# A one-core decode kernel: the query weights split into two loads, and the MLP weights issued from another engine's queue

## The chip, the cores and the metric

The kernel runs on one core of a Trainium2 chip. The metric is the device time of one launch in microseconds (us); three runs of the kernel before gave 1302.87, 1302.97 and 1303.05 us, median 1302.97. All times below that carry a position ("at 31.44") are counted from the first instruction of the profiled execution.

## The reference

One decode step for two sequences (B = 2) with model width 512:

```
xn  = layernorm(x)                                  # x: [2, 1, 512]
q   = (xn @ wq) -> 32 heads of 128                  # wq: [512, 4096], 8.4 MB
s   = softmax(q k^T / sqrt(128)) v, then @ wo       # k, v: [2, 8 kv heads, 32768, 128]
g   = silu( relu(xn @ w1 + b1)^2 @ w2 + b2 )        # w1: [512, 1792], w2: [1792, 512]
out = x + s * g
```

Everything is float32. The key and value caches are 537 MB together; wq is 8,388,608 bytes, w1 and w2 together 7,340,032, wo 8,388,608. Each byte is read once.

## The kernel before, in words

**Buffers.** Two slots of 128 partitions x 16384 floats (8.4 MB each) take the large loads in turn. A load is one DMA of 128 rows, one row for each partition. The output weights wo have their own buffer, `wo_sb`.

**The stream of loads.** All large loads are issued by SyncE (the row name is SPq) through `load` (L164 to L171), in this order: wq into slot 0, wm (w1 and w2 side by side, 14336 floats to a row) into slot 1, and then for each of the 16 pairs of sequence and kv head two key loads (`kt`) and two value loads (`vt`), 64 loads of 8.4 MB in all, which alternate between the slots. At the end follow six pieces of wo. The first two loads need no wait (L173). Every later one waits until TensorE has read the slot's previous contents: `release` (L178) records TensorE's token and calls `load` for the next entry of the list, so the order in which TensorE finishes with the slots is the order in which SyncE issues. Load i+2 is thus issued when load i has been consumed, while load i+1 is on its way.

**Ahead of the stream.** Behind the first two loads SyncE runs `AHEAD` = 9 semaphore clears on a semaphore that is not yet in use (L174), which move its later instructions by nine places and do nothing else.

**The front of the program**, in TensorE's order: layernorm in a few small matmuls; q = xn @ wq as 32 matmuls (L252 to L258: 4 blocks d of 128 rows of wq, each with 8 matmuls into two PSUM banks), which wait for the whole of wq; the release of slot 0, which lets SyncE issue the first key load; transposes of q; then `mlp` (L295), which waits for wm, does 16 + 14 matmuls with VectorE work between them, and releases slot 1, which lets SyncE issue the second key load. Each float32 matmul shows as two records in the profile, so the 32 matmuls of q are x64 there.

**ScalarE** issues three tiny loads at the start (`small`, and `xb` twice), does one copy and a square root for the layernorm (L244), and then waits for TensorE's 32 matmuls before it copies q out of PSUM (L262).

**The loop** runs over the 16 pairs on TensorE, ScalarE and VectorE: scores from two key loads, softmax, and the value products from two value loads. TensorE's work for one load takes about 9 us. `release` is called at the end of each load's matmuls (L291, L384).

Tokens are pairs of a semaphore and a value; `wait` (L42) puts a wait ahead of the engine's next instruction. `fetch` (L58) is a DMA issued by the engine itself, in its own order of instructions. Every operation of TensorE, ScalarE and VectorE is recorded by one helper, so they all carry L64 in the profile.

Of the kernel before, what the change touches and what calls it, by code (L numbers as in the profile page):

```python
# [16 lines left out]
B, D, HQ, HKV, SK, DH, F = 2, 512, 32, 8, 32768, 128, 1792  # L17
REP = HQ // HKV
NS = B * HKV
ND = D // P  # L20
# [5 lines left out]
FJ = FG // 32  # L26
SLOT = HALF
NSLOT = 2
PIECES = (16, 8, 5, 2)
WIDE = 24  # L30
AHEAD = 9
HN = P // 2
SCALE = 1.0 / math.sqrt(DH)

# [91 lines left out]
def build(nc, x22, x8, kt, vt, wq, wm, wo, out):  # L126
    pe, act, dve = (Looped(nc, e, n) for e, n in ((nc.tensor, "pe"), (nc.scalar, "act"), (nc.vector, "dve")))
    pool, sp = (Engine(nc, e, n) for e, n in ((nc.gpsimd, "pool"), (nc.sync, "sp")))

    def mm(*args, **kw):  # L130
        pe.do("matmul", *args, **kw)
# [4 lines left out]
    def sb(name, *shape):  # L136
        return nc.alloc_sbuf_tensor(name, [P, *shape], F32)

    slots = [sb(f"slot{i}", SLOT) for i in range(NSLOT)]
# [10 lines left out]
    small, xs, xc, sq, st = sb("small", P), sb("xs", 22), sb("xc", 8), sb("sq", 8), sb("st", 16)  # L150
# [5 lines left out]

    slot_sem = [nc.alloc_semaphore(f"slot{i}") for i in range(NSLOT)]
    piece_sem = [nc.alloc_semaphore(f"piece{i}") for i in range(len(PIECES) + 2)]
    small_sem, xe_sem, out_sem = (nc.alloc_semaphore(n) for n in ("small", "xe", "out"))
    count = [0] * NSLOT  # L160
    free = [None] * NSLOT
    issued = [0]

    def load(src, width):  # L164
        i = issued[0] % NSLOT
        issued[0] += 1
        if free[i] is not None:
            sp.wait(free[i])
        count[i] += 16
        nc.sync.dma_start(slots[i][:, 0:width], src).then_inc(slot_sem[i], 16)  # L170
        return i, (slot_sem[i], count[i])  # L171

    stream = [load(wq, SLOT), load(wm, 2 * FJ * D)]  # L173
    for _ in range(AHEAD):  # L174
        nc.sync.sem_clear(out_sem)
    todo = [(x[s, u], SLOT) for s in range(NS) for x in (kt, vt) for u in range(2)]
# [16 lines left out]
    t = pool.done(g.memset(ident[:, :], 0.0))  # L193
# [12 lines left out]
    for u in range(2):  # L206
# [5 lines left out]
    t = dve.done("tensor_reduce", selh[:, :], ident[:, :].rearrange("p (a h) -> p h a", h=REP), axis=AX.X, op=ALU.add)  # L212
    dve.wait(t)
    t_seln = dve.done("tensor_scalar", seln[:, :], selh[:, :], -SCALE, None, op0=ALU.mult)
    t_selg = dve.done("tensor_reduce", selg[:, :].rearrange("p (r y) -> p r y", r=2),
                      ident[:, None, :].to_broadcast([P, 2, P]).rearrange("p r (g y) -> p r y g", g=NG), axis=AX.X, op=ALU.add)
# [6 lines left out]
    t = pe.done()  # L223
    dve.wait(t)
    t = dve.done("tensor_copy", xs[:, :], ms[:, 0:22])
    pe.wait(t, t_one)
    mm(ms[:, 32:40], mean[:, :], xs[:, 0:8], start=True, stop=True)
    t = pe.done()
    dve.wait(t)
    t = dve.done("tensor_reduce", st[:, 2:4], ms[:, 32:40].rearrange("p (d b) -> p b d", b=B), axis=AX.X, op=ALU.add)  # L230
    dve.wait(t)
    t = dve.done("tensor_tensor", xc[:, :].rearrange("p (d b) -> p d b", b=B), xs[:, 0:8].rearrange("p (d b) -> p d b", b=B),
                                 st[:, None, 2:4].to_broadcast([P, ND, B]), op=ALU.add)
    dve.wait(t)
    t = dve.done("tensor_mul", sq[:, :], xc[:, :], xc[:, :])
    pe.wait(t)
    mm(ms[:, 64:72], mean[:, :], sq[:, :], start=True, stop=True)
    t = pe.done()
    dve.wait(t)
    t = dve.done("tensor_reduce", st[:, 4:6], ms[:, 64:72].rearrange("p (d b) -> p b d", b=B), axis=AX.X, op=ALU.add)  # L240
    dve.wait(t)
    t = dve.done("tensor_scalar", st[:, 6:8], st[:, 4:6], -1.0, 1e-5, op0=ALU.mult, op1=ALU.add)
    act.wait(t)
    t = act.done("activation", st[:, 8:10], st[:, 6:8], AF.Sqrt)  # L244
    dve.wait(t)
    t = dve.done("reciprocal", st[:, 10:12], st[:, 8:10])
    dve.wait(t)
    t_x = dve.done("tensor_tensor", xT[:, :, 0:B], xc[:, :].rearrange("p (d b) -> p d b", b=B),
                                   st[:, None, 10:12].to_broadcast([P, ND, B]), op=ALU.mult)


    i, t = stream[0]  # L252
    pe.wait(t_x, t, t_selg)
    for d in range(ND):
        for f in range(2):
            for c in range(NG):
                lo = d * HQ * DH + (f * NG + c) * W
                mm(sc[f][32 * c:32 * c + 32, :], xT[:, d, :], slots[i][:, lo:lo + W], start=(d == 0), stop=(d == ND - 1))  # L258
    t = pe.done()
# [3 lines left out]
    for f in range(2):  # L263
# [3 lines left out]
        t = pe.done()  # L267
# [14 lines left out]
    def scores(u):  # L282
        i, t = stream[0]
        pe.wait(t, t_set, t_exp[u])
        for j in range(NJ):
            for c in range(NG):
                lo = (c * NJ + j) * W
                mm(sc[u][32 * c:32 * c + 32, :], qz[:, 28 - 4 * j:60 - 4 * j], slots[i][:, lo:lo + W],
                         start=(j == 0), stop=(j == NJ - 1))
        t = pe.done()  # L290
        release(t)  # L291
        dve.wait(t)
        return t, dve.done("tensor_reduce", rm[:, u:u + 1], sc[u][:, :], axis=AX.X, op=ALU.max)
# [44 lines left out]
    for s in range(NS):  # L338
# [4 lines left out]
        t_s, t = scores(1)  # L343
# [3 lines left out]
        t = dve.done("tensor_reduce", r1[:, :], rm[:, :], axis=AX.X, op=ALU.max)  # L347
        pe.wait(t, *([t_rs] if t_rs else []))
        tr(ms[:, :P], r1[:, :].to_broadcast([P, P]), ident[:, :])
        t = pe.done()  # L350
        dve.wait(t)
        t = dve.done("tensor_reduce", mh[:, :], ms[:, :P].rearrange("p (a h) -> p h a", h=REP), axis=AX.X, op=ALU.max)
        dve.wait(t)
        t = dve.done("tensor_mul", mm4[:, :], mh[:, :], seln[:, :])
        dve.wait(t)
        t = dve.done("tensor_reduce", nm[:, :], mm4[:, :], axis=AX.X, op=ALU.add)
# [5 lines left out]
        for u in range(2):  # L362
# [3 lines left out]
            t = pe.done()  # L366
# [4 lines left out]
        t = pe.done()  # L371
        dve.wait(t)
        t_rs = dve.done("reciprocal", rs[:, :], ms[:, :REP])
        for u in range(2):
            i, t = stream[0]
            pe.wait(t, t_pT[u], t_osb)
            for n in range(32):
                y = n % NG
                k, r = divmod(n, 8)
                lo = k * 32 + r * 4  # L380
# [7 lines left out]
        for n in range(4):  # L388
            lo = n * (P - REP)
# [19 lines left out]
    first = True  # L409
# [8 lines left out]
    for n, sem in zip(PIECES, piece_sem):  # L418
        if h == WIDE:
            pe.wait(t_w)  # L420
            for u in range(2):
                for c in range(NG):
                    lo = c * P + u * HN
                    mm(acc[32 * c:32 * c + 32, 0:2 * HN:2], selg[:, 32 - u:64 - u], o_sb[:, lo:lo + HN], start=(u == 0), stop=False)
        pe.wait((sem, 16))
        for h in range(h, h + n):
            if h < WIDE:
                c = h % NG
                mm(wb[32 * c:32 * c + 32, :], heads(h, 0), wt[:, h, :], start=(h < NG), stop=(h >= WIDE - NG))
                if h == WIDE - 1:  # L430
                    t = pe.done()
# [12 lines left out]
    t = pe.done()  # L444
    dve.wait(t, t_gate)
    t = dve.done("tensor_tensor_scan", yb[:, :], gate[:, :], acc[:, :2 * HN], 0.0, op0=ALU.mult, op1=ALU.add)
    sp.wait(t)
    nc.sync.dma_start(out, yb[:, :]).then_inc(out_sem, 16)
    used = sorted(x.num for x in [e.sem for e in (pe, act, dve, pool, sp)] + slot_sem + piece_sem + [small_sem, xe_sem])
    nc.sync.sem_clear(range(used[0], used[-1] + 1))  # L450
    nc.sync.wait_ge(out_sem, 16)
    for e in (pe, act, dve):
# [48 lines left out]
```

## Time and profile before

| | before |
|---|---|
| median of three runs | 1302.97 us |
| the profiled execution's own time | 1302.98 us |
| its span, first to last instruction | 1301.7 us |
| DMA queue of SyncE (q1) | 10512 packets, 561.06 MB, busy 99.7% of 16 engines' span |
| DMA queue of ScalarE (q10) | 65 packets, 0.02 MB |
| instruction queue q8 | 5 packets, 0.08 MB |
| TensorE busy | 672.9 us (52%) |
| VectorE, ScalarE, GpSimd busy | 49.5, 79.1, 5.6 us |

The core has 16 DMA engines. A queue's share is the time that its packets took, over 16 spans. A "row" of a load below is the part of one partition, 64 KB for a full slot. The page's chain names what each engine waited for last; the DMA issue rows tell how long after its issue a load had landed.

### The profile page before, as it was taken

What the parts mean: (1) busy time and instruction counts of PE and PEld (TensorE: products, weight loads), DVE (VectorE), ACT (ScalarE), POOL (GpSimd) and SP (SyncE); (2) the same over time, 40 slices, a digit from 0 to 9 for tenths busy, and PEclk for the clock granted to TensorE, in tenths of its full rate; (3) what the DMA queues carried; (4) which work ended last, traced back from release to release, by engine and by line L of the source; (5) the groups of instructions that cost most, each with busy time, mean ns of one, the idle gap of its engine ahead of it and who ended that gap; (6) DMA issues with size and microseconds to landing.
All of it is one profiled execution on the core that took longest, in us unless ns stands there. A gap on an engine that the chain in (4) does not pass through costs nothing.

```text
span 1301.7 us, 10377 instructions
## 1 busy us (share of the span) xinstructions
PE 672.9 (52%) x4713; PEld 208.6 (16%) x4713; DVE 49.5 (4%) x165; ACT 79.1 (6%) x139; POOL 5.6 (0%) x30
## 2 busy tenths in 40 slices
PE   3445445535536545545645545554654654554565
PEld 1111111211112111111211111121111211111122
DVE  0000000000000000000000000000000000000000
ACT  1010010100001010010101001010010101001010
POOL 0000000000000000000000000000000000000000
PEclk9777677678677778667677767767767767767777
DMA  9999999999999999999999999999999999999998
GB/s 412 428 446 425 443 425 445 419 443 427 429 441 427 443 427 443 423 445 421 443 427 427 443 427 443 427 443 421 445 423 441 429 427 443 427 443 425 445 421 363
DMA packets 10583, 561.17 MB, mean 431 GB/s; under 512 B 1195, under 2 KB 1617, under 8 KB 1745
## 3 DMA queue, kind: packets, MB, share of 16 engines
q1 hardware_dynamic: 10512, 561.06, 99.7%
q8 instruction: 5, 0.08, 0.0%
q10 hardware_dynamic: 65, 0.02, 0.0%
q14 instruction: 1, 0.01, 0.0%
HBM read 561.01 MB, written 0.07 MB: 431 GB/s over the span
## 4 chain that ended last, share of the span: by engine, by line
DMA 75%; PE 24%; issue 1%; DVE 0%; ACT 0%; SPq 0%; ACTq 0%
DMA slot<-in_vt 36%; DMA slot<-in_kt 36%; PE sc L64 12%; PE o_ps L64 11%; DMA slot<-in_wm 3%; PE wb L64 1%; DVE hT L64 0%; ACT o_sb L64 0%; DVE o_sb L64 0%; PE ot L64 0%; DVE yb L64 0%; SPq L170 0%; ACT sc L64 0%; ACTq L454 0%; ACTq L102 0%
## 5 line engine op out<-in xcount | busy, mean ns | idle before, releaser
L64 PE MATMUL sc<-slot,qz 128*32 128x512 f32 x2048 | 295.5, 742 | 299.6 <-DMA slot<-in_kt 299.6
L64 PE MATMUL o_ps<-slot,pT 128*16 128x512 f32 x2048 | 294.4, 739 | 209.0 <-DMA slot<-in_vt 209.0
L64 PEld LDWEIGHTS sc<-slot,qz 128*32 128x32 f32 x2048 | 81.0, 133 | 503.3 <-issue 503.3
L64 PEld LDWEIGHTS o_ps<-slot,pT 128*16 128x16 f32 x2048 | 69.3, 113 | 420.7 <-issue 420.7
L64 ACT ACT_TABLE_LOAD x19 | 24.4, 1283 | 650.3 <-DVE nm L64 647.3
L64 PE MATMUL tp<-ident,prob 128*128 128x128 f32 x136 | 31.2, 403 | 53.2 <-ACT prob L64 53.2
L64 DVE TENSOR_REDUCE rm<-sc 128x1 f32<-128x512 f32 x32 | 22.1, 691 | 574.9 <-PE sc L64 574.9
L64 ACT COPY o_sb<-o_ps 128x512 f32<-128x512 f32 x16 | 9.4, 586 | 504.8 <-PE o_ps L64 504.8
L64 PEld LDWEIGHTS tp<-ident,prob 128*128 128x128 f32 x136 | 24.0, 206 | 57.7 <-issue 55.7
L64 DVE TENSOR_REDUCE t<-ot 128x4 f32<-128x64 f32 x16 | 3.6, 224 | 524.2 <-PE ot L64 524.2
L64 ACT ACTIVATE prob<-sc,nm 128x512 f32<-128x512 f32 x32 | 21.7, 683 | 0.2
L64 ACT COPY pT<-tp 128x512 f32<-128x512 f32 x32 | 18.8, 586 | 13.8 <-PE tp L64 13.8
L64 PE MATMUL sc<-slot,xT 128*32 128x512 f32 x64 | 8.6, 695 | 17.7 <-DMA slot<-in_wq 17.7
L64 PE MATMUL ot<-ident,o_sb 128*128 128x128 f32 x64 | 10.1, 280 | 13.7 <-ACT o_sb L64 12.8
L64 PEld LDWEIGHTS ms<-selh,l 128*128 128x128 f32 x64 | 15.6, 334 | 0.0
L64 PE MATMUL ms<-ident,r 128*128 128x128 f32 x16 | 4.7, 294 | 20.0 <-DVE r L64 20.0
L64 PE MATMUL ms<-selh,l 128*128 128x4 f32 x64 | 13.7, 319 | 0.0
L64 PEld LDWEIGHTS ot<-ident,o_sb 128*128 128x128 f32 x64 | 6.7, 141 | 27.9 <-issue 27.9
L64 PE MATMUL wb<-slot,xT 128*32 128x448 f32 x32 | 4.8, 762 | 6.4 <-DMA slot<-in_wm 6.4
L275 POOL COPY qz<-qT 128x4 f32<-128x4 f32 x16 | 3.0, 187 | 1167.2 <-PE sc L64 1137.2
L64 PEld LDWEIGHTS ms<-ident,r 128*128 128x128 f32 x16 | 2.1, 133 | 34.1 <-issue 34.1
L64 ACT ACTIVATION_READ_ACCUMULATOR prob<-sc,nm 128x1 f32 x32 | 6.3, 196 | 0.0
(63 smaller groups left out, 55.4 us busy)
## 6 DMA issues: line engine op xcount, KB each, us to landing
slot<-in_wm SPq DMA_DIRECT2D x1, 7168.0 KB, 38.4
wo_sb<-in_wo SPq DMA_DIRECT2D x1, 4096.0 KB, 39.1
wo_sb<-in_wo SPq DMA_DIRECT2D x1, 2048.0 KB, 43.5
wo_sb<-in_wo SPq DMA_DIRECT2D x1, 1280.0 KB, 45.8
slot<-in_kt SPq DMA_DIRECT2D x32, 29.1
slot<-in_vt SPq DMA_DIRECT2D x32, 29.1
wo_sb<-in_wo SPq DMA_DIRECT2D x1, 512.0 KB, 46.6
wo_sb<-in_wo SPq DMA_DIRECT2D x2, 128.0 KB, 46.4
```

The lines of the kernel that those rows point to most:

```text
L64: instruction = getattr(self.e, name)(*[x(i) if callable(x) else x for x in args], **kw)
L275: return pool.done(g.tensor_copy(qz[:, 28:32], qT[:, b, hkv, :]))
```

## The change

wq is loaded in two parts into the same slot: the first 12288 floats of each row (`FIRST`, the blocks d = 0 to 2) with a semaphore of its own, `first_sem`, and the last 4096 floats (block d = 3) with slot 0's semaphore. Both are issued by SyncE, one behind the other. The load wm, which SyncE issued second, is now issued by ScalarE: behind the square root, ScalarE waits until the first part of wq has landed and then issues wm into slot 1. TensorE waits for `first_sem` ahead of its first 24 matmuls and for slot 0's semaphore ahead of the last 8. SyncE runs 8 semaphore clears in place of 9. The 64 cache loads and the pieces of wo stay as they were, on SyncE.

```diff
-AHEAD = 9
+AHEAD = 8
+FIRST = 3 * SLOT // 4
...
-    stream = [load(wq, SLOT), load(wm, 2 * FJ * D)]
+    for lo, hi, sem in ((0, FIRST, first_sem), (FIRST, SLOT, slot_sem[0])):
+        nc.sync.dma_start(slots[0][:, lo:hi], wq[:, lo:hi]).then_inc(sem, 16)
+    stream = [(i, (slot_sem[i], 16)) for i in range(2)]
+    issued[0] = 2
+    count[0:2] = 16, 16
     for _ in range(AHEAD):
         nc.sync.sem_clear(out_sem)
...
     t = act.done("activation", st[:, 8:10], st[:, 6:8], AF.Sqrt)
+    act.wait((first_sem, 16))
+    act.fetch(slot_sem[1], slots[1][:, 0:2 * FJ * D], wm)
...
-    pe.wait(t_x, t, t_selg)
+    pe.wait(t_x, (first_sem, 16), t_selg)
     for d in range(ND):
+        if d == ND - 1:
+            pe.wait(t)
         for f in range(2):
```

SyncE's instructions at the start of its program, before:

```order
L170 DMA slot<-in_wq 128x16384 [waits barrier_Pool_Activation_PE_DVE_SP_release]
L170 DMA slot<-in_wm 128x14336
L175 ISA x9
L170 DMA slot<-in_kt 128x16384 [waits pe] x2
L170 DMA slot<-in_vt 128x16384 [waits pe] x2
```

and now (the lines are those of the changed file):

```order
L175 DMA slot<-in_wq 128x12288 [waits barrier_Pool_Activation_PE_DVE_SP_release]
L175 DMA slot<-in_wq 128x4096
L180 ISA x8
L171 DMA slot<-in_kt 128x16384 [waits pe] x2
L171 DMA slot<-in_vt 128x16384 [waits pe] x2
```

The load of wm has left SyncE's order, the load of wq has become two, and one clear (ISA) is gone; the cache loads follow as before.

ScalarE's instructions from the layernorm to the gate of the MLP, before:

```order
L64 ACTIVATE st<-st 128x2 [waits dve]
L64 COPY prob<-sc 128x512 [waits pe]
L64 COPY prob<-sc 128x512
L64 COPY o_sb<-wb 128x512 [waits pe]
L64 ACT_TABLE_LOAD
L64 ACTIVATE gate<-yb 128x64 [waits dve]
```

and now:

```order
L65 ACTIVATE st<-st 128x2 [waits dve]
L65 DMA slot<-in_wm 128x14336 [waits first]
L65 COPY prob<-sc 128x512 [waits pe]
L65 COPY prob<-sc 128x512
L65 COPY o_sb<-wb 128x512 [waits pe]
L65 ACT_TABLE_LOAD
L65 ACTIVATE gate<-yb 128x64 [waits dve]
```

Between the square root (`ACTIVATE st`) and the copies of q (`COPY prob`) stands the load of wm, with a wait for the first part of wq.

TensorE's instructions around the query projection (`sc<-slot,xT`), before:

```order
L64 MATMUL ms<-sq,mean 128x8 [waits dve]
L64 MATMUL sc<-slot,xT 32x512 [waits slot0,dve]
L64 MATMUL sc<-slot,xT 32x512 x31
L64 MATMUL tp<-ident,prob 128x128 [waits act]
L64 MATMUL tp<-ident,prob 128x128 x3
```

and now:

```order
L65 MATMUL ms<-sq,mean 128x8 [waits dve]
L65 MATMUL sc<-slot,xT 32x512 [waits first,dve]
L65 MATMUL sc<-slot,xT 32x512 x23
L65 MATMUL sc<-slot,xT 32x512 [waits slot0]
L65 MATMUL sc<-slot,xT 32x512 x7
L65 MATMUL tp<-ident,prob 128x128 [waits act]
L65 MATMUL tp<-ident,prob 128x128 x3
```

The one wait for wq has become two, 24 matmuls behind the first and 8 behind the second; the matmuls themselves and their order are the same.

More of the change, by code (lines that the diff above doesn't have):

```diff
@@ L158, in build @@
     piece_sem = [nc.alloc_semaphore(f"piece{i}") for i in range(len(PIECES) + 2)]
-    small_sem, xe_sem, out_sem = (nc.alloc_semaphore(n) for n in ("small", "xe", "out"))
+    small_sem, xe_sem, first_sem, out_sem = (nc.alloc_semaphore(n) for n in ("small", "xe", "first", "out"))
     count = [0] * NSLOT
@@ L448, in build @@
     nc.sync.dma_start(out, yb[:, :]).then_inc(out_sem, 16)
-    used = sorted(x.num for x in [e.sem for e in (pe, act, dve, pool, sp)] + slot_sem + piece_sem + [small_sem, xe_sem])
+    used = sorted(x.num for x in [e.sem for e in (pe, act, dve, pool, sp)] + slot_sem + piece_sem + [small_sem, xe_sem, first_sem])
     nc.sync.sem_clear(range(used[0], used[-1] + 1))
```

## The prediction

> **What bounds the kernel now.** I read the DMA rows of the page first, since a kernel that reads 561 MB once can hardly be bound by anything else.
>
> ```profile
> span 1301.7 us, 10377 instructions
> DMA  9999999999999999999999999999999999999998
> q1 hardware_dynamic: 10512, 561.06, 99.7%
> q8 instruction: 5, 0.08, 0.0%
> HBM read 561.01 MB, written 0.07 MB: 431 GB/s over the span
> DMA 75%; PE 24%; issue 1%; DVE 0%; ACT 0%; SPq 0%; ACTq 0%
> ```
>
> The 16 DMA engines are busy for 99.7% of the span with SyncE's queue alone. The chain gives TensorE 24%, but that is the release of one slot while the other slot's load flows. What is left is 0.3% of 1301.7, 3.9 us. The timeline shows where a gain could still lie.
>
> ```profile
> 0.74 0.38 SPq L170 DMA_DIRECT2D slot<-in_wq  x1
> 1.18 0.44 SPq L170 DMA_DIRECT2D slot<-in_wm  x1
> 22.82 8.56 PE L64 MATMUL sc<-slot,xT 128*32 128x512 f32 x64 [17.66 <-DMA slot<-in_wq]
> 31.44 19.13 SPq L170 DMA_DIRECT2D slot<-in_kt  x2
> 39.67 4.80 PE L64 MATMUL wb<-slot,xT 128*32 128x448 f32 x32 [6.45 <-DMA slot<-in_wm]
> 60.43 8.53 PE L64 MATMUL sc<-slot,qz 128*32 128x512 f32 x64 [9.11 <-DMA slot<-in_kt]
> 79.68 9.14 PE L64 MATMUL sc<-slot,qz 128*32 128x512 f32 x64 [10.72 <-DMA slot<-in_kt]
> 1279.75 9.83 PE L64 MATMUL o_ps<-slot,pT 128*16 128x512 f32 x64 [10.08 <-DMA slot<-in_vt]
> 1300.07 0.35 SPq L448 DMA_DIRECT2D out<-yb  x1
> ```
>
> TensorE starts on a load as it lands. From the first key load (60.43) to the last value load (1279.75) there are 63 loads of 8.389 MB: 19.354 us each, 433.4 GB/s, 27.1 GB/s for an engine. At that rate a row of 64 KB takes an engine 2.42 us, a row of wm (56 KB) 2.12, a 16 KB row 0.605. Every stage of the front runs at this rate but one:
>
> ```profile
> 22.80:39.67 16.87, 9.70 (x73) 3.24 (x73) 0.38 (x2) 1.07 (x2) 0.19 (x1) 0.89 1.02 443
> 39.67:60.43 20.76, 8.86 (x77) 2.42 (x78) 2.28 (x7) 2.13 (x3) 0.00 (x0) 0.75 0.95 409
> 60.43:79.68 19.25, 8.53 (x65) 2.37 (x66) 0.69 (x1) 0.00 (x0) 0.00 (x0) 0.77 1.00 432
> 99.30:1279.75 1180.45, 614.28 (x4160) 187.92 (x4161) 40.77 (x135) 67.34 (x120) 2.62 (x14) 0.72 1.00 433
> ```
>
> These are stretches, with their length, each engine's busy time, the granted TensorE clock, the DMA share and GB/s. The stretch of the first key load is 20.76, 1.41 over 19.354. The DMA view of 40 to 60 us has the cause in it:
>
> ```profile
> DMA packets 146, 8.42 MB, mean 421 GB/s; under 512 B 16, under 2 KB 16, under 8 KB 16
> q1 hardware_dynamic: 144, 8.39, 97.2%
> q8 instruction: 2, 0.03, 0.6%
> ```
>
> SyncE's 144 packets are 128 rows of 64 KB and 16 closing writes under 512 B: a row is one packet, 8 to an engine. Two 16 KB packets of instructions also pass. A load has landed only when its slowest engine is done, so an engine that carries one such packet delays the landing by 1.41 us, and two packets on two engines delay it no more than one.
>
> **The change part by part.** Against the profiled execution's 1302.98 us (span 1301.7 and 1.3 around it; the median of the runs is 1302.97):
>
> *The bytes* are the same, and so is the first issue at 0.74. What precedes the first byte and what follows the last landing is not touched.
>
> *One load more.* wq's last quarter travels in 128 rows of 16 KB and adds 8 packets to an engine. Two pieces of wo bound their price:
>
> ```profile
> 1250.15 2.12 SPq L185 DMA_DIRECT2D wo_sb<-in_wo  x4
> wo_sb<-in_wo SPq DMA_DIRECT2D x1, 4096.0 KB, 39.1
> wo_sb<-in_wo SPq DMA_DIRECT2D x1, 2048.0 KB, 43.5
> ```
>
> The 2048 KB piece (16 KB rows) lands 4.4 us longer after its issue than the one ahead of it, and was issued some 0.53 later (2.12 for four): 4.93 us against 4.84 at the steady rate. I take +0.1 us.
>
> [...]
>
> *Part one of wq* lands 2.097 MB earlier: TensorE starts at 22.82 - 4.84 = 17.98 in place of 22.82. ScalarE, idle at that place since its square root, issues wm at about 18.0. When do its bytes flow? In the DMA view of the first 4 us (40 slices of 0.1)
>
> ```profile
> GB/s 0 0 0 0 0 0 0 0 0 0 0 0 0 0 0 0 0 51 1992 1321 1971 1321 1976 1311 0 655 0 0 0 0 0 0 0 0 0 0 0 0 0 0
> out<-yb SPq DMA_DIRECT2D x1, 64.0 KB, 1.6
> ```
>
> wq, issued at 0.74, starts at 1.8 on the first engine and by 2.6 on the last: 1.1 to 1.9 after the issue. `out` lands 1.6 after its issue; less 1.1 and 0.15 of bytes, some 0.35 lies between last byte and landing. So wm flows from 19.1 to 19.9. The rest of wq has flowed since about 17.3, by then 3 to 4 of its 8 rows on an engine, and one is under way: 3 to 5 are left.
>
> *Two queues at once.* How they share an engine is the open part. The three tiny loads of ScalarE are the nearest rows (DMA views of 4 to 9, 9 to 14 and 14 to 20 us):
>
> ```profile
> q10 hardware_dynamic: 8, 0.00, 0.3%
> q10 hardware_dynamic: 16, 0.00, 0.4%
> q10 hardware_dynamic: 8, 0.00, 0.1%
> ```
>
> They were issued by 2.9 and go by in groups of eight over 10 us, behind rows of wq. I read that as turns by packet. Then each left row of wq is followed by a row of wm (0.605 + 2.12 = 2.72 us), and its closing write by one more: with 4 rows, 19.5 + 0.6 + 4 x 2.72 + 2.1 + 0.35 = 33.4 (30.7 with 3, 36.2 with 5) in place of 22.7.
>
> [...]
>
> TensorE has done its first 48 records at about 24.9 and idles. After such a pause it restarts slowly:
>
> ```profile
> 24.50 0.23 PEld L64 LDWEIGHTS sc<-slot,xT 128*32 128x32 f32 x4 [0.62 <-issue]
> 25.36 0.23 PEld L64 LDWEIGHTS sc<-slot,xT 128*32 128x32 f32 x4 [0.62 <-issue]
> 29.05 0.14 PEld L64 LDWEIGHTS sc<-slot,xT 128*32 128x32 f32 x4 [0.29 <-issue]
> 29.48 0.14 PEld L64 LDWEIGHTS sc<-slot,xT 128*32 128x32 f32 x4 [0.29 <-issue]
> ```
>
> Four records take 0.86 us early and 0.43 later. The last 16 records take 16 x 0.215 = 3.4. The first key load is issued at 33.4 + 0.1 + 3.4 = 36.9 (34.2 to 39.7) in place of 31.44, and flows 1.1 to 1.9 later, at 38.0 to 38.8. The engines have wm until about 39.67 - 0.45 = 39.2, whichever order the same bytes take. So they do not run dry: cost 0, with a lower bound of 0 and an upper one of 41.6 - 39.2 = 2.4 us with five rows left. I take 0, as four rows are the middle.
>
> *wm lands later*, since key rows now share with its last ones: at most two turns of 2.42 on 39.67, 44.5.
>
> ```profile
> 39.67 4.86 PE wb L64 x32
> 50.24 29.31 DMA slot<-in_kt
> 79.56 0.12 issue
> ```
>
> From wm to the release of its slot it is 50.24 - 39.67 = 10.57, so the second key load is issued by 55.1 and flows by 57.0. The first key load keeps the engines busy until 60.43 - 0.47 = 60.0 on the slowest, 58.6 on those without an instruction packet. Cover 1.6 us at worst; cost 0. From there on the stream is the one before.
>
> *The other edits*: ScalarE's wait holds up only the copies of q, which wait for TensorE's last 16 records anyway. One clear fewer on SyncE falls into its idle time ahead of 31.44. Both 0.
>
> Sum: 1302.98 + 0.1 = **1303.1 us**, no change.
>
> **The rivals.**
>
> *A gap at each change of queue.* For: an instruction packet cost 1.41 us where its 16 KB are 0.605, so 0.8 for two changes, 0.4 each. Against: on its way wq met ScalarE's packets, yet took 22.82 - 0.74 = 22.08; less 19.354 and the 1.6 of `out`, 1.1 are left, and at four packets on each of eight engines that is at most 0.14 a change. An engine changes queue some 12 times (four rows and a closing write, twice each, and two for the key rows). That makes 0 to 1.7 us by the tiny loads and 4.8 by the instruction packets: 1307.9. It decides above 0.22 a change. I hold the tiny loads nearer, as they too go from HBM to SBUF.
>
> *The queues share evenly by bytes instead of by packet.* wq's rest would land at about 24.1, the first key load be issued at 26.6 and take half the rate from wm, of whose 459 KB an engine has 174 by 28. The other 285 KB take 21 us: landing 49.4, release 60.0, next bytes at 61.1 to 61.9, while the engines ran dry at 58.6. About 3 us: 1306.1. It decides if wm lands after 47. Against: the groups of eight.
>
> *wq's rest is starved for longer*, to the end of wm: landing 39.6, first key load issued at 43.1, bytes at 44.2 to 45.0 against 39.2, some 5.5 us: 1308.6. It needs all 8 rows to be left, where the head start gives at most 5.
>
> *A gain*: two busy queues hide what an instruction packet costs beyond its bytes, or fill the start. Even 1.4 us, the whole of the delay, gives 1301.7, still no change by the bound below. A gain of 2.6 us would need the 23 us with two queues to run 11% above 433 GB/s; no stretch does.
>
> **How the numbers follow.** 0.2% is 2.6 us, about what a measurement of this kernel can tell from no change. No change has 0.77: the forecast (0.68), a gap per change below 0.22 (0.05), the small gain (0.04). Slower has 0.20: gaps of 0.22 to 0.4 (0.12), sharing by bytes (0.04), the starved rest (0.04). Faster has 0.03, for a rate with two queues that this trace doesn't show. The range starts at the small gain, 1301.7, and reaches towards the gap's case, to 1306.5, leaving out some 0.13; the forecast's own range is 1302.4 to 1304.5.
>
> **What would show it.** The changed profile should have TensorE's first query matmuls at 18, its last ones in a row of their own at 31 to 36 behind a wait for wq, the first key load issued at 34 to 40, wm's matmuls at 40 to 45, and then 60.4 for the first key load's matmuls as before. If these start at 65, gaps or a dry engine took the time; if the second key load is issued after 57, wm was shared too long. The forecast is wrong if this row moves by more than 2.6 us, or if the 19.35 between later loads does.

## The result, and the profile after

The changed kernel takes 1306.7 us (median of 7 runs, 1306.37 to 1308.92) against 1302.97: a ratio of 1.0035, 95% interval 1.0025 to 1.0045. It is slower by 3.7 us, outside the range, and its runs fall into two groups, at 1306.4 to 1306.7 and at 1308.4 to 1308.9, where the kernel before stays within 0.3 us. The profile is of a run in the upper group: 1308.66 us, span 1307.2.

The page of the changed kernel, in the rows that were read first before:

```profile
span 1307.2 us, 10377 instructions
DMA  9899999999999999999999999999999999999998
q1 hardware_dynamic: 10512, 553.72, 98.0%
q10 hardware_dynamic: 209, 7.36, 1.3%
```

The two queues together are now busy for 99.3% of a span that is 5.5 us longer, and the missing part stands in the second of the 40 slices. The timeline of that place:

```profile
17.87 0.36 ACTq L65 DMA_DIRECT2D slot<-in_wm  x1
17.98 7.79 PE L65 MATMUL sc<-slot,xT 128*32 128x512 f32 x48 [12.72 <-DMA slot<-in_wq]
27.02 1.93 PE L65 MATMUL sc<-slot,xT 128*32 128x512 f32 x16 [1.25 <-DMA slot<-in_wq]
29.01 33.48 SPq L171 DMA_DIRECT2D slot<-in_kt  x2
49.40 5.29 PE L65 MATMUL wb<-slot,xT 128*32 128x448 f32 x32 [18.60 <-DMA slot<-in_wm]
56.80 5.32 PE L65 MATMUL wb<-slot,hT 128*32 128x512 f32 x28 [2.10 <-DVE hT L65]
85.47 9.89 PE L65 MATMUL sc<-slot,qz 128*32 128x512 f32 x64 [14.41 <-DMA slot<-in_kt]
1285.31 9.00 PE L65 MATMUL o_ps<-slot,pT 128*16 128x512 f32 x64 [10.91 <-DMA slot<-in_vt]
```

wm, which had landed at 39.6, now lands at 49.4. The first key load is issued earlier than before (29.01 against 31.44) and the second much later: the merged row of two issues begins at 29.01 and lasts 33.48, and the chain puts the second at 62.16 (50.24 before).

```profile
17.87 31.48 DMA slot<-in_wm
62.16 23.19 DMA slot<-in_kt
```

The DMA view of 58 to 64 us shows in 40 slices of 0.15 us when packets start:

```profile
GB/s 0 0 0 0 0 0 0 0 0 0 0 0 0 0 0 0 0 0 0 0 0 0 0 0 0 0 0 0 0 0 0 0 0 0 3495 1311 437 437 437 874
q1 hardware_dynamic: 32, 1.05, 51.8%
```

No row starts between 58.0 and 63.1. The key load on its way was the only one left, its last rows had started, and the next one could not be issued before the mlp had freed slot 1. Its first bytes come 1 us after its issue, and its first rows are slow: 16 rows (the other 16 packets are the closing writes of the load before) take 51.8% of 6 us on 16 engines, 3.1 us each in place of 2.42. By stretches:

```profile
27.02:49.40 22.38, 3.07 (x25) 1.26 (x25) 0.39 (x2) 1.07 (x2) 0.19 (x1) 0.64 1.01 439
49.40:63.98 14.58, 11.04 (x76) 2.86 (x77) 2.06 (x6) 1.80 (x2) 0.00 (x0) 0.74 0.71 284
104.92:1285.30 1180.38, 609.04 (x4159) 186.75 (x4160) 40.81 (x135) 67.27 (x120) 2.61 (x14) 0.74 1.00 433
```

While two queues are busy (27 to 49) the engines move 439 GB/s; most of the loss is in the stretch behind, at 284; from the first value load on, 1180.38 us against 1180.45, the kernel is the one before. The second key load is used at 85.47 in place of 79.68, 5.79 later; the last value load at 1285.31 in place of 1279.75, 5.56 later; next to nothing is made up on the way.

### The profile page after: what moved, and what is told of

It is laid out like the page before. It is cut to its first block, busy times and chain, and to the rows that moved or that the text cites. A ratio compares the mean times of both kernels' runs of the same rounds, so it can differ in the third digit from the quotient of the medians.

```text
span 1307.2 us, 10377 instructions
## 1 busy us (share of the span) xinstructions
PE 670.1 (51%) x4713; PEld 208.5 (16%) x4713; DVE 49.6 (4%) x165; ACT 79.0 (6%) x139; POOL 5.5 (0%) x30
## 4 chain that ended last, share of the span: by engine, by line
DMA 76%; PE 23%; issue 0%; DVE 0%; SPq 0%; ACT 0%
DMA slot<-in_kt 35%; DMA slot<-in_vt 34%; PE sc L65 12%; PE o_ps L65 11%; DMA wo_sb<-in_wo 3%; DMA slot<-in_wm 2%; DMA slot<-in_wq 1%; PE wb L65 1%; DVE hT L65 0%; DVE o_sb L65 0%; ACT o_sb L65 0%; SPq L190 0%; DVE yb L65 0%; SPq L171 0%
## 5 line engine op out<-in xcount | busy, mean ns | idle before, releaser
L65 PE MATMUL sc<-slot,qz 128*32 128x512 f32 x2048 | 292.0, 734 | 297.8 <-DMA slot<-in_kt 297.0
L65 PE MATMUL wb<-slot,hT 128*32 128x512 f32 x28 | 5.3, 864 | 2.1 <-DVE hT L65 2.1
```

Source lines behind the costliest of these rows:

```text
L65: instruction = getattr(self.e, name)(*[x(i) if callable(x) else x for x in args], **kw)
```

## The experiments

Each edit is against the changed kernel. Theory A says: wm on its own queue takes turns with the first key load, lands ten us late, the mlp frees slot 1 too late for the second key load, and the engines run dry.

**The split alone.** wm goes back to SyncE, behind the two parts of wq.

```diff
+    nc.sync.dma_start(slots[1][:, 0:2 * FJ * D], wm).then_inc(slot_sem[1], 16)
...
-    act.wait((first_sem, 16))
-    act.fetch(slot_sem[1], slots[1][:, 0:2 * FJ * D], wm)
```

> The split alone: wq in two parts with TensorE's two waits, but wm issued by SyncE behind them, as before the change. Theory A (the changed kernel loses its time because wm, on a second queue, takes turns with the first key load and lands at 49.4, so the second key load is issued too late): one queue, so wm lands at about 39.6 again, the mlp frees slot 1 at about 50.2 and nothing runs dry; 1303.0 us, within 0.5 of the kernel before. Theory B (the split itself, the additional 16 KB rows or the earlier release of slot 0, costs time): 1305 us or more.

Measured: 1302.9 us (ratio 1.0, 0.9991 to 1.001). In its profile the first key load is issued as early as 27.65 and wm still lands at 39.4:

```profile
27.65 25.00 SPq L171 DMA_DIRECT2D slot<-in_kt  x2
39.48 5.37 PE L65 MATMUL wb<-slot,xT 128*32 128x448 f32 x32 [10.04 <-DMA slot<-in_wm]
```

On one queue the key load stood behind wm and took none of its turns: wm landed at 39.4, where it landed at 49.4 with the key load on another queue. The split and the early release cost nothing that shows (1302.9 us against 1302.97); theory B, a price of the split itself, falls.

**The move alone.** wq in one load with TensorE's single wait, as before the change; wm issued by ScalarE behind it.

```diff
-    for lo, hi, sem in ((0, FIRST, first_sem), (FIRST, SLOT, slot_sem[0])):
-        nc.sync.dma_start(slots[0][:, lo:hi], wq[:, lo:hi]).then_inc(sem, 16)
+    nc.sync.dma_start(slots[0][:, 0:SLOT], wq).then_inc(slot_sem[0], 16)
...
-    act.wait((first_sem, 16))
+    act.wait(stream[0][1])
...
```

> The move to ScalarE's queue alone: wq in one load, wm issued by ScalarE behind its landing. Theory A: the engines run dry for some 2 us at 22.3, between wq's last byte and wm's first; wm flows from 24, the first key load, issued at 31.4, takes turns with wm's last 4 rows, wm lands at 52 to 54, the second key load is issued at 63 to 66 and the engines are dry again for 4 to 6 us: 1309 to 1311.5 us. Theory B (the split is at fault): about 1303 to 1305 us, the first gap alone.

Measured: 1309.74 us (1306.16 to 1311.88; ratio 1.005, 1.0035 to 1.0066). The median is in theory A's range, the scatter is wider than it. wm is issued at 22.64 and lands at 49.54, earlier than the 52 to 54 expected, and the second key load is issued at 63.09:

```profile
22.64 26.90 DMA slot<-in_wm
63.09 23.51 DMA slot<-in_kt
```

So the move costs without the split too. Whether it costs more than with it can't be told from five runs whose range takes in most of the changed kernel's; and the two differ in one thing more, since wm is issued here when the engines have nothing left of wq.

**wm in a buffer of its own.** wm is loaded into `wo_sb`, which is empty until the end; slot 1 is free from the start, and the second key load is issued right behind the first.

```diff
-    act.fetch(slot_sem[1], slots[1][:, 0:2 * FJ * D], wm)
+    act.fetch(wm_sem, wo_sb[:, 0:2 * FJ * D], wm)
...
     release(t)
+    stream.append(load(*todo.pop(0)))
```

> The changed kernel with wm loaded into the buffer of wo, which is empty until the end, so that slot 1 is free from the start and the second key load is issued right behind the first. wm still goes through ScalarE's queue and takes turns with the key rows. Theory A: wm still lands at about 49, but no load waits for it; the gap at 58 to 63 goes, 1303.0 us within 0.5 of the kernel before, in each run. Theory C (two busy queues cost engine time at each change of queue): the loss stays, 1306 us or more.

Measured: 1302.89 us (1302.76 to 1302.98 in 10 runs; ratio 0.9999, 0.999 to 1.0009). wm lands as late as in the changed kernel, and the second key load is used at 79.72 as in the kernel before:

```profile
49.39 4.83 PE L65 MATMUL wb<-wo_sb,xT 128*32 128x448 f32 x32 [18.61 <-DMA wo_sb<-in_wm]
79.72 8.88 PE L65 MATMUL sc<-slot,qz 128*32 128x512 f32 x64 [10.87 <-DMA slot<-in_kt]
```

This is the run that decides: the same two queues, the same turns, the same late wm, and no loss once no load waits for it. Theory C, a price for each change of queue, falls; with about a dozen changes on an engine, by the prediction's count, the whole difference to the kernel before is within 0.1%.

**The first key load held back until wm has landed.**

```diff
     t = pe.done()
+    sp.wait((slot_sem[1], 16))
     release(t)
```

> The changed kernel with one wait more on SyncE: the first key load is issued only when wm has landed. Theory A: wm has the engines to itself and lands at about 39.7, the key load's first bytes come 1.1 to 1.9 us after its issue, the engines are dry for 1.6 to 2.5 us there and the second key load, issued at 50 to 52, comes in time: 1305.3 us (1304.5 to 1306). Theory C, or any loss that has nothing to do with the key load's issue: the time of the changed kernel plus this gap, 1308 us or more.

Measured: 1305.37 us (1305.05 to 1305.48; ratio 1.0018, 1.0009 to 1.0028), the value that theory A gave. wm lands at 39.55, and a wait more makes the changed kernel faster:

```profile
39.56 12.90 SPq L171 DMA_DIRECT2D slot<-in_kt  x2
39.59 5.08 PE L65 MATMUL wb<-slot,xT 128*32 128x448 f32 x32 [8.93 <-DMA slot<-in_wm]
62.94 9.21 PE L65 MATMUL sc<-slot,qz 128*32 128x512 f32 x64 [9.73 <-DMA slot<-in_kt]
```

**A smaller first part**, so that wm starts with more of wq left, wq's rest takes turns with wm for longer, and the first key load comes later. Two sizes, the second wait moved to the right block:

```diff
-FIRST = 3 * SLOT // 4
+FIRST = SLOT // 2          # the other kernel: 5 * SLOT // 8
```

> The first part of wq is half of it instead of three quarters; TensorE's second wait stands ahead of block d = 2. ScalarE issues wm at about 13; counting from the changed kernel's profile, wm's first rows come 3.5 us later, at 16.6 to 17.6, when 4 of wq's 8 remaining rows (32 KB) are left. Theory A: they take turns, wq's rest lands at about 33, the first key load is issued at 37 to 38.5 and shares nothing or one row with wm, which lands at 39.7 to 42: 1303.0 to 1304.3 us. Theory C (two busy queues cost time): as long with two queues as in the changed kernel, so 1306 us or more.

> The first part of wq is five eighths; TensorE's second wait stands in the middle of block d = 2. By the same count wm's first rows come at about 19 with 3 of wq's rows (24 KB) left, wq's rest lands at about 31, the first key load is issued at 35 to 36 and shares at most one or two rows with wm, which lands at 39.7 to 44.5. Theory A: the second key load comes in time, 1303.0 us within 0.5. Theory C: 1306 us or more.

Measured: 1304.98 us with a half (1303.86 to 1305.71; ratio 1.0016, 1.0007 to 1.0025), 1303.18 with five eighths (1302.93 to 1303.96; ratio 1.0003, 0.9994 to 1.0012). The profile with five eighths:

```profile
36.50 15.75 SPq L171 DMA_DIRECT2D slot<-in_kt  x2
39.56 4.91 PE L65 MATMUL wb<-slot,xT 128*32 128x448 f32 x32 [1.27 <-DMA slot<-in_wm]
```

This is the regime that the prediction had described for three quarters: the key load issued at 36.5, wm landing undisturbed, no loss. With a half the key load is issued at 38.45, too late for wm's end: it is first used at 62.27 in place of 60.43. About 2 us go there, 0.7 more than the upper end of what was expected. Between too early (29.01: wm landed at 49.35) and too late (38.45: the first key load was used 1.84 us later than before) lies 36.50, which cost nothing that shows.

**The two groups.** The changed kernel was run again as it is, and with eight matmuls that keep TensorE busy in the mlp's pause.

> The changed kernel unchanged, for its two groups of times (1306.4 to 1306.7 and 1308.4 to 1308.9 us). Theory D (the groups differ by the TensorE clock granted during the mlp, whose second batch of matmuls took 5.3 us in the profiled run and 3.6 before): both groups again; a profile from the lower group has that batch at about 3.6 us and the second key load issued about 2 us earlier. Theory E (they differ by one more turn of a key row ahead of wm's end): a profile from the lower group has wm landing at about 47 in place of 49.4.

> The changed kernel with eight additional matmuls between the mlp's two batches, where TensorE waits 2.1 us for VectorE; they write a PSUM bank that nobody reads there. Theory D: TensorE is busy over the pause and keeps its clock, the second batch takes about 3.6 us in every run, and only the lower group is left, 1306.0 to 1306.9 us (where the eight matmuls themselves run at the slow clock they take 3.4 us and delay the batch by 1.3). Theory E: both groups stay.

Measured: again two groups, 1306.35 once and 1307.95 to 1308.52 four times; the profile is from the upper one, with wm landing at 49.3 and a second batch of 5.3 us. The eight matmuls were mis-sized: 128 columns wide, they took 7.13 us instead of 1.7 and held up the second batch, 1311.17 us. They can't show what the kept clock is worth, but the run says something on the groups. There are still two, 1309.4 to 1309.5 (two runs) and 1311.2 to 1312.1 (three). The profile is from the lower one, and in it wm lands at 46.8, though nothing ahead of that had been changed in the program:

```profile
26.85 2.82 PE L66 MATMUL sc<-slot,xT 128*32 128x512 f32 x16 [2.18 <-DMA slot<-in_wq]
29.70 33.67 SPq L172 DMA_DIRECT2D slot<-in_kt  x2
46.80 5.58 PE L66 MATMUL wb<-slot,xT 128*32 128x448 f32 x32 [14.48 <-DMA slot<-in_wm]
```

TensorE's last 16 query records took 2.82 us, where the changed kernel's profile has 1.93, at a granted clock of 1.00. So the first key load was issued 0.7 us later, at 29.70, and wm's sixth row went ahead of the first key row. The DMA views of 29 to 33 us, the changed kernel first (two rows), then this one:

```profile
q10 hardware_dynamic: 19, 1.09, 62.8%
q1 hardware_dynamic: 13, 0.85, 49.1%
q10 hardware_dynamic: 32, 1.84, 105.9%
```

In the changed kernel 13 of the 16 engines start a key row behind wm's fifth row, and three wm's sixth; here all 16 start wm's fifth and sixth. The other profiles with wm on its own queue and a first part of three quarters agree (the kernel with the key load held back aside): with the key load issued at 28.86 to 29.01 wm lands at 49.2 to 49.4, with 29.70 to 30.68 at 46.8 to 46.9.

The next pair was made with the key load one microsecond later, and with narrow matmuls:

```diff
-    release(t)
     act.wait(t)
     t_q = [act.done("copy", prob[:, f, :], sc[f][:, :]) for f in range(2)]
+    sp.wait(t_q[1])
+    release(t)
...   (the other kernel, behind the mlp's first batch; BUSY = 8)
+        pe.wait(t_oT)
+        for n in range(BUSY):
+            c = n % NG
+            mm(ot[32 * c:32 * c + 32, :], ident[:, 0:32], oT[:, 0:W], start=True, stop=True)
```

> The changed kernel with the first key load issued one microsecond later: SyncE waits for ScalarE's second copy of q instead of TensorE's matmuls, so it issues at about 30.1 in place of 29.0. Theory E (the two groups of times are one turn more or less of a key row ahead of wm's closing writes, decided by whether the first key row comes ahead of or behind wm's sixth row): it now always comes behind it, wm lands at about 46.8 in every run, and the later issue makes the kernel faster: one group, 1306.0 to 1306.8 us. Theory D (the granted clock during the mlp makes the groups): two groups 2 us apart as before, 1306.5 and 1308.5 or both some us lower.

> The eight additional matmuls again, 32 columns wide in place of 128, since the wide ones took 7.1 us in place of the 1.7 I had counted on. They should take 1.7 us (3.4 at the slow clock) in the pause of 2.1. Theory D: the mlp's second batch takes 3.6 us in each run and there is one group, at 1306.5 us or below. Theory E: the second batch takes 3.6 us, so both groups come down by up to 1.7 us, and there are still two of them, 2 us apart: about 1304.7 to 1305 and 1306.7 to 1307.

Measured: 1306.12 us for the later key load (nine of 11 runs at 1305.7 to 1306.5, two at 1303.9 and 1304.2; ratio 1.0022, 1.0013 to 1.0031), 1306.64 for the narrow matmuls (nine runs at 1306.4 to 1307.4, two at 1304.6; ratio 1.0027, 1.0018 to 1.0036). The chains of the two profiles, the later key load first:

```profile
17.77 29.07 DMA slot<-in_wm
46.89 5.74 PE wb L65 x32
54.68 5.35 PE wb L65 x28
60.05 22.89 DMA slot<-in_kt
```

```profile
17.73 31.49 DMA slot<-in_wm
49.26 5.14 PE wb L66 x32
56.45 3.65 PE wb L66 x28
60.12 23.16 DMA slot<-in_kt
```

Each brings the second key load's issue forward by 2.0 to 2.1 us against the changed kernel's 62.16, by another way. In the first, the first key load is issued at 30.68 (1.7 us later, as TensorE's last 16 records took 2.60 us there), and wm lands 2.5 us earlier, one turn of a 64 KB row, and the second batch is as slow as ever. In the second, wm lands at 49.2 and the batch takes 3.65 in place of 5.35. Behind the turn stand wm's closing writes. In the changed kernel 3 of the 16 pass at 45.9 to 46.5 and 13 only at 48.3 to 49.1 (DMA views of these two windows):

```profile
q10 hardware_dynamic: 3, 0.00, 0.3%
q10 hardware_dynamic: 13, 0.00, 0.9%
```

Behind the slow batch stands the granted clock: 1.00 through the pause itself (54.7 to 56.8), 0.54 in 56.8 to 60.5, where the batch runs, and 1.00 behind that; with the narrow matmuls 1.00 while it runs (the number ahead of the last two in each row).

```profile
56.80:60.50 3.70, 3.70 (x20) 1.02 (x24) 0.00 (x0) 0.00 (x0) 0.00 (x0) 0.54 0.04 18
60.50:62.20 1.70, 1.62 (x12) 0.23 (x4) 0.00 (x0) 0.03 (x1) 0.00 (x0) 1.00 0.00 0
```

```profile
56.45:60.10 3.65, 3.62 (x28) 0.91 (x28) 0.00 (x0) 0.00 (x0) 0.00 (x0) 1.00 0.05 18
```

What sets the clock from run to run was not shown. After the same pause of 2.10 us the batch took 5.32 us in the changed kernel (56.80) and 3.63 in the kernel with wm in a buffer of its own, without any matmuls added and with wm landing at the same 49.35:

```profile
56.32 3.63 PE L65 MATMUL wb<-wo_sb,hT 128*32 128x512 f32 x28 [2.10 <-DVE hT L65]
```

Both kernels still show two groups, about 2 us apart. Theory E had expected a single one for the later key load, theory D a single one for the narrow matmuls, so neither theory alone accounts for both; for the narrow matmuls the two groups lie about where theory E had put them. Two single runs of the unchanged kernel were meant to catch its lower group in a profile:

> The changed kernel once more, for a profile from its lower group of times (4 of 7 and 1 of 5 runs so far). Theories D and E both move the release of slot 1 by about 2 us, and either could make the lower group. At about 1306.5 us: D alone has wm landing at 49.3 and the mlp's second batch taking 3.6 us; E alone has wm landing at 46.8 and that batch taking 5.3 us; both together would give about 1304.3. At about 1308.5: 49.3 and 5.3 again.

> As the run before it, for a second profile: 1306.5 us with wm landing at 49.3 and a second batch of 3.6 us (D), or with 46.8 and 5.3 us (E); or 1308.5 us with 49.3 and 5.3.

Measured: 1308.72 and 1308.48 us, both upper, with wm landing at 49.2 and a second batch of 5.35 us. Last, both remedies at once:

> The later key load and the narrow matmuls together. If the turn ahead of wm's closing writes (2.4 us) and the clock of the mlp's second batch (about 2 us) are separate delays of the same release and add up: wm lands at 46.8, the second batch takes 3.6 us, slot 1 is free at about 58.0, the engines are hardly dry: 1303.9 to 1304.6 us, with a run at 1303 where wm has one turn fewer still. If they are one effect seen twice: no better than the 1306.1 and 1306.6 us of each alone.

Measured: 1303.8 us (eight of 11 runs at 1303.5 to 1304.0, three up to 1305.04; ratio 1.0009, 1.0 to 1.0018).

```profile
17.81 29.07 DMA slot<-in_wm
46.92 4.64 PE wb L66 x32
53.60 3.65 PE wb L66 x28
57.27 23.05 DMA slot<-in_kt
```

The two delays are separate and add up: the second key load's issue comes 4.9 us earlier than in the changed kernel's profile, 2.5 by wm's landing, 1.7 by the second batch and 0.7 by the first (4.64 against 5.35), where each remedy alone gave 2.0 to 2.1. The profiles in which that issue comes behind 56.7 fit a single rule, a fit and not worked out: the run is late by about as much as the issue is later than some 56.7 us. It is 62.16 at 1308.66 us, 60.05 at 1306.25, 60.12 at 1306.45, 57.27 at 1303.53. (The kernel with half of wq in the first part and the one with the key load held back lose their time at the first key load, and the rule says nothing of them.) Which of the two delays is the one that is missing in the changed kernel's own lower group stays open, as no profile from it could be had. Either would bring its 2 us, and each has been seen to be missing by itself: the turn in the profile with the wide matmuls, the slow clock in the one with wm in a buffer of its own.

No version beat the kernel before: the best, 1302.89 and 1302.9, are equal to it.

## Why the prediction was wrong

**What held.** The bound is the DMA engines, busy for 99.7% of the span before and 99.3% in the changed kernel, and no run showed a gain. Part one of wq released TensorE at 17.98, as worked out; that it agrees to the hundredth is chance, as three more profiles of the same kernel have 17.86 to 17.90. The two queues took turns by packet: in 32 to 46 us of the changed kernel's DMA view both have 48 packets, of 3.15 and 2.75 MB.

```profile
q1 hardware_dynamic: 48, 3.15, 51.8%
q10 hardware_dynamic: 48, 2.75, 45.3%
```

The changes of queue cost nothing that shows (1302.89 us with wm in a buffer of its own). The extra rows of 16 KB, put at 0.1 us, do not show either (1302.9 us with the split alone).

**The step that failed** is "wm flows from 19.1 to 19.9 ... 3 to 5 are left". In the DMA view of 17 to 22 us (slices of 0.125 us)

```profile
GB/s 131 1180 131 393 393 131 1180 131 524 131 262 1049 262 393 131 262 1049 262 393 131 655 655 393 262 131 786 524 393 262 131 918 393 393 262 131 3801 459 1376 1376 459
q1 hardware_dynamic: 130, 1.87, 87.2%
q10 hardware_dynamic: 16, 0.92, 42.3%
```

wm's large rows start in the 36th slice, at 21.4: 3.5 us after the issue, not 1.1 to 1.9. By then all but about one of wq's eight rows on an engine had started (1.87 of 2.10 MB in this window). I took the time from issue to first byte from wq's own issue, which met an idle engine; on an engine with a queue already busy the newcomer waited longer. Counted with 3.5 us instead, wq's rest was expected at about 33 and 31 for the two smaller first parts, and TensorE waited for it until 33.13 and 31.09. Why the wait is 3.5 us the runs do not show. The trace of before held what may be a hint, quoted and not used: ScalarE's tiny loads were issued by 2.9, yet only 8 of their packets pass in 4 to 9 us.

From there the error ran on, each term in the same direction. wq's rest landed before 27.02 (predicted 33.4). TensorE's last 16 records took 1.93 us (predicted 3.4; it had idled for 1.25 us, and the granted clock was 1.00). So the first key load was issued at 29.01 (predicted 36.9, range from 34.2), and its first rows came from 32.5 on, with three rows of wm still to go on most engines. It took a turn ahead of each of them, and another ahead of the closing write, where I had allowed two turns in all. wm landed at 49.35 (at the latest 44.5). The mlp then took 62.16 - 49.40 = 12.76 us where I had carried over 10.57 as a constant: its second batch now met a clock of 0.54 and took 1.7 us longer, its first 0.5. The cover that I had put at 1.6 us at worst was overrun by 3 to 4.5 us: bytes at 63.1, against engines that run out at 58.6 to 60.0. Another 0.7 us went into the second key load's slow first rows; the last part of the 5.79 us, 0.6 us or more, is not accounted for.

**The rivals.** The outcome is the second rival, wm landing after 47 because the first key load shares with it for too long, at a chance of 0.04. It has the sign, the place and, for the median, nearly the time (1306.1 against 1306.7). That its landing of 49.4 is the measured one is luck, since it was worked out from a key load issued at 26.6 and another way of sharing: I had tied it to sharing by bytes, as if turns by packet ruled it out. Turns by packet were enough with the key load issued at 29.01. The threshold, wm landing after 47, held where the second batch took 3.65 us (1303.8 us with wm landing at 46.9, 1306.64 with 49.2), not where it took 5.35 (1306.12 us with wm landing at 46.9); I tested it against one arithmetic of the key load's issue instead of asking over what range of issue times it would be crossed. With the issue at 29 in place of 36.9 it takes four turns of 2.42 us, a sum that I could have written down.

The rival of a gap at each change of queue was given three times that chance, 0.12, and no run shows such a gap.

## What to carry to other kernels

In the changed kernel wm, on the second queue and issued first, was not served first: the first key load, issued 11.14 us behind it, took every other packet from it (48 of the 96 in 32 to 46 us), and wm landed at 49.35 in place of 39.6. So before a load is moved to another queue, ask who waits for its landing and what else will be issued until then. In a stream where each issue waits for a slot's release, the margin is the time from the release to the moment when the load on its way has passed; work it out for the earliest and for the latest issue of each neighbour, not for one. And a path carried over from a profile as a constant (the mlp's 10.57 us, 12.76 in the changed kernel) may contain a piece that differs with the clock granted at that moment (the second batch: 3.65 us at 1.00, 5.35 where it was 0.54 at first).

## What the runs showed of the hardware

- wm's first row started 3.5 us after its issue with the other queue busy (17.87 to 21.4) against 1.1 us on idle engines (the first load: 0.74 to 1.8). For the first key load it was again 3.5 us (29.01 to 32.5).
- wm's closing writes went by behind a row of the other queue: one 64 KB row more ahead of them put its landing off by 2.5 us (46.9 or 49.3).
- Which of the two it was went with 0.7 us in the issue of the other load: 29.01 or 29.70.
- Holding back a load made the kernel faster: 1306.12 us with the first key load 1.7 us later, 1305.37 with it ten microseconds later, against 1306.7 and 1308.2 without (medians).
- The first rows of a load on engines that had run dry took 3.1 us each in place of 2.42 (the second key load, from 63.1 on).
- TensorE's second mlp batch took 3.65 or 5.35 us for the same 28 records, at a granted clock of 1.00 or of 0.54 at first, after the same pause of 2.1 us. With eight narrow matmuls in the pause it took 3.65 in both profiles; it did so in the kernel before and with wm in a buffer of its own too, without them.
